# Expert weight loads spread over eight pairs, a second bank in the product chain of the last super block, and a new order in its first pair and routing

## The chip, the core and the metric

The kernel runs on one core of a Trainium2 chip. The metric is device time in microseconds (us) of one execution. The core's engines run side by side: TensorE (PE; its weight loads are shown as PEld), VectorE (DVE), ScalarE (ACT), GpSimd (POOL) and SyncE (SP), from which every transfer is issued, in one queue. PSUM has eight banks here, `bank[0]` to `bank[7]`, each 128 x 512 fp32.

## The reference

Three layers, one after the other, on 4 x 768 = 3072 tokens of 512 features:

```python
# attention: 8 heads of 64, chunks of 32 queries; each chunk sees 8 memory keys and a window of 56
scores = scale * np.matmul(q_c, k_full.transpose(0, 1, 3, 2))
a = np.exp(scores - np.max(scores, axis=-1, keepdims=True))
a = a / (np.sum(a, axis=-1, keepdims=True) + 1e-09)
out[:, :, c_start:c_end] = np.matmul(a, v_full)
# dense layer, 512 -> 2048 -> 512
r = np.maximum(x @ w_in, 0.0)
y = (s * (r * r) + b) @ w_out
# soft mixture, 8 experts of 4 slots, 512 -> 1024 -> 512
logits = y @ phi
d = softmax(logits, axis=0); slot_input = d.T @ y
slot_out[e] = np.maximum(slot_input[e] @ w1[e], 0.0) @ w2[e]
out = softmax(logits, axis=1) @ slot_out
```

(`softmax` stands for the lines that subtract the maximum, exponentiate and divide by the sum.) All is fp32.

## The kernel before

The 3072 tokens are six blocks of 512. Features lie on partitions, the tokens of a block on the free axis. Each fp32 operand of a large product is split into a high and a low part, and one product is three matmuls (high x high, high x low, low x high), all 128 x 128 by 128 x 512.

**Plain steps.** Blocks 0 and 1 run in 16 steps each, one 128-wide tile of the hidden layer a step: `mm_h` (12 matmuls, L332) into one of two banks, `make_g` (relu on ACT, times `s` on DVE, plus `b` on ACT, low part on DVE), then `mm_y` of the step before (`mm_job`, 12 matmuls, L351): three matmuls into each of four banks, which visits the banks in turn, four matmuls a round. The attention of later blocks runs between these as background tasks (`bg`, `run_bg`): `qk` (scores into a bank, then softmax on DVE and ACT), `tr` (transposes) and `pv`. The last four steps (`hand_step`) have their order written out.

**Super blocks.** Blocks 2 and 3, and 4 and 5, are done two at a time by `super_block(s, pending)`, s = 0 and 1, with seven products in place of eight (a 2 x 2 scheme over two blocks, two halves of the features and two hidden tiles). A *pair* p, 0 to 7, stands for hidden tiles p and p + 8. In it PE does, in this order:

- `a11` into bank A, copied by ACT to `c11`; `s1` into C, copied to `c22` (`y1n`, second half); `s2` accumulated on A, copied to `c12` (`y1n`, first half);
- in the first super block, `pv` of one attention unit in bank B and `qk` of the next in D;
- the first pending output job, 12 matmuls into the four banks `yp`;
- `s4` on C, added by DVE to `c12` (L768); `s3` on A, added by DVE to `c22` (L773); then relu (ACT, L677) and a 1024-wide multiplication (DVE, L680) make the hidden values of the second token block, which are kept for later;
- up to two routing tasks of the block before, in banks D and B: logits (`log`), transposes of y (`ytr0` to `ytr3`), of the exponents (`etr`), slot sums (`slot`); in pair 3 also `csoft`, a small softmax on DVE and ACT alone;
- the second pending job, 12 matmuls;
- `a22` on A, from which ACT and DVE make `t21` (`rt0n`, L677, L680); `a12` into B, which DVE adds to `c11` (L803), and `t11` follows; in the first super block then four transposes of the next attention unit into D.

Each product is six matmuls (`prod`, L662). The two jobs of a pair's own values are put on the pending list and run in the next pair; `finish(p - 1)`, at the start of the next pair, makes the last of those values, `G[0]`. The next pair's `a11` goes into A again, so it cannot start before `t21` has been made from A. Banks A, B, C, D are `yq`, `bank[4:8]` for s = 0 and `bank[0:4]` for s = 1; `yp` are the other four.

At the start `pending` holds what is left over: for s = 0 the last plain step's `mm_y` and the evacuation of `YB` (`evac_spare`, L372 on ACT and L370 on DVE, two banks each), for s = 1 the last two output jobs of s = 0, the second followed by an evacuation.

After the pairs, 16 output jobs of the second token block (`t2_job`) run into `yq`, with the routing of the first block between them. The first of the 16 visits the banks in the order D, C, A, B, one matmul each, three rounds.

**Transfers.** In the first super block the split operands of the products are also stored to DRAM (`wc_store`, `DWC`), and in the second they are loaded from there (`wc_load`, L617: `wi0n`, `wi1n`, `w14n`, `w15n`), five loads a pair with the weights of the output jobs (L602), each issued when its tile has been read for the last time. The expert weights (`e_load`, L494 and L496) are 64 loads of 512 KB in a fixed order, each started by `e_free` of some tile that is no longer needed. At the end of pair 0 of the second super block 13 tiles are freed at once, so 13 of these loads stand in SP's queue one behind the other, ahead of the pair's next loads.

PE's and SP's order is the order of the code throughout; that of ACT, DVE and POOL also, from the last four plain steps to the end of the super blocks.

Of the kernel before, what the change touches and what calls it, by code (L numbers as in the profile page):

```python
# [11 lines left out]
AF = mybir.ActivationFunctionType  # L12
# [4 lines left out]
NB = 6  # L17
# [21 lines left out]
def tile_attention_moe_softmoe(  # L39
# [287 lines left out]
    def mm_h(n, kts):  # L327
        w = WI[n % 2].rearrange("p (a k c) -> p a k c", a=2, k=4)
        for kt in kts:
            x = hl(X[(n // NF) % 2][kt])  # L330
            for i, (a, b) in enumerate(((0, 0), (0, 1), (1, 0))):
                pe.matmul(HB[n % 2], lhsT=r32(w[:, a, kt, :]), rhs=r32(x[:, b]),  # L332
                          start=(kt == 0 and i == 0), stop=(kt == 3 and i == 2))

    def make_g(n):
        r, t = hl(RT[n % 2])[:, 0], hl(RT[n % 2])[:, 1]
        g = hl(G[n % 2])
        act.activation(out=r, in_=HB[n % 2], func=AF.Relu, scale=1.0 / WSCALE ** 2)  # L338
        dve.scalar_tensor_tensor(out=t, in0=HB[n % 2], scalar=s_col, in1=r, op0=ALU.mult, op1=ALU.mult)  # L339
        act.activation(out=r32(g[:, 0]), in_=t, func=AF.Identity, bias=b_col)  # L340
        dve.scalar_tensor_tensor(out=r32(g[:, 1]), in0=t, scalar=b_col, in1=g[:, 0], op0=ALU.add,  # L341
                                 op1=ALU.subtract)

    def mm_job(yb, wt, gt, first, last, dts=(0, 1, 2, 3)):
        w, g = hl(wt), hl(gt)
        order = [(i, dt) for i in range(3) for dt in dts]
        if last:
            order.sort(key=lambda o: o[1])
        for i, dt in order:
            a, b = ((0, 0), (1, 0), (0, 1))[i]  # L350
            pe.matmul(yb[dt], lhsT=r32(w[:, a, dt * 128:dt * 128 + 128]), rhs=r32(g[:, b]),  # L351
                      start=(first and i == 0), stop=(last and i == 2))
# [27 lines left out]
    def y_logits(j, b):  # L380
        logit_mm(b)
        L = b[:, 0:128]
        old, new = mrun[(j + 1) % 2], mrun[j % 2]
        act.activation(out=lts, in_=L, func=AF.Copy)
        dve.tensor_reduce(out=new if j == 0 else st["mj"], in_=L, axis=AX.X, op=ALU.max)
        if j:
            dve.tensor_tensor(out=new, in0=st["mj"], in1=old, op=ALU.max)
            dve.tensor_tensor(out=st["da"], in0=old, in1=new, op=ALU.subtract)
            act.activation(out=st["aa"], in_=st["da"], func=AF.Exp)
        dve.tensor_scalar(out=st["nm"], in0=new, scalar1=-1.0, scalar2=None, op0=ALU.mult)  # L390
        act.activation(out=ets, in_=L, func=AF.Exp, bias=st["nm"],
                       accum_out=st["sj"] if j else srun)
        if j:
            dve.scalar_tensor_tensor(out=srun, in0=srun, scalar=st["aa"], in1=st["sj"], op0=ALU.mult,
                                     op1=ALU.add)

# [122 lines left out]
    for tasks in bg.values():  # L519
        tasks.sort(key=lambda t: t[0] != "pv")  # L520

    def run_bg(task, a, b=None):
        if task == "qk":
            att_qk(a, b)
            if a + 2 < NB * NHP:
                load_q(a + 2)
                load_k(a + 2)
            att_exp(a, b)
# [8 lines left out]
        elif task == "log":  # L537
            y_logits(a, b)
        elif task[:3] == "ytr":
# [139 lines left out]
    def times(out, h, r):  # L679
        dve.scalar_tensor_tensor(out=out, in0=h, scalar=s_col, in1=r, op0=ALU.mult, op1=ALU.mult)  # L680

    def super_block(s, pending):
        j1 = NPL + 2 * s
        yp, yq = (bank[0:4], bank[4:8]) if s == 0 else (bank[4:8], bank[0:4])
        A, B, C, D = yq
        ch = [fresh("y0"), fresh("y1")]
# [3 lines left out]
        jr = j1 - 1  # L690
        routing = {1: ("log", "ytr0"), 2: ("etr", "ytr1"), 3: ("ytr2", "ytr3"), 4: ("slot",)}
        gring = ["sp4", "sp5", "g1", "g0"] * 4
# [15 lines left out]

        def t2_job(i, dts=(0, 1, 2, 3)):
            mm_job(yq, cur[WR[i]], cur[gring[i]], i == 0, i == NF - 1, dts)  # L710

# [14 lines left out]
        for p in range(NPR):  # L726
            c11 = hl(ch[0])[:, p % 2]
            more = p + 1 < NPR
            prod(A, "a11", "b11", p)
            act.activation(out=c11, in_=A, func=AF.Copy)  # L730
            if s == 0 and p == 0:
                x_split("t4", 0, 1)
            if p:
                if s == 0:
                    att_place(4 * NHP + p, D)
                finish(p - 1)
            if s == 0:
# [19 lines left out]
            if s == 0:  # L757
                if p:
                    run_bg("pv", 4 * NHP + p, B)
                if more:  # L760
                    run_bg("qk", 4 * NHP + p + 1, D)
            pending.pop(0)()
            if p or s == 0:
                next_load(p, 0) if p else ws_load(R[3], 1)
            else:
                ws_load(R[2], NPR + 1)
# [5 lines left out]
            prod(A, "s3", "t3", p, False)  # L772
            dve.tensor_tensor(out=c22, in0=A, in1=c22, op=ALU.add)  # L773
            relu(r2, ch[1])
            times(cur[G2[p]], ch[1], r2)
            w_prep(2, p + 1)
            if not more:
                t2_load(4)
                prep(1)
                if s == 0:  # L780
                    x_split("t1", 1, 0)
                    x_split("t1", 1, 1)
            for i, t in enumerate(routing.get(p, ())):
                run_bg(t, jr, (D, B)[i])
            if p == 3:
                run_bg("csoft", jr)
            pending.pop(0)()
            if p:
                next_load(p, 1)
            elif s:  # L790
                ws_load(R[3], 1)
# [4 lines left out]
            relu(t21, A)  # L796
            times(t21, A, t21)
            prod(B, "a12", "b21", p)
            if s:
# [11 lines left out]
            pending.append(lambda p=p: mm_job(yp, cur[R[(2 * p + 1) % 4]], G[0], False, p == NPR - 1))  # L811
            if s and p == 0:
                for t in [cur[f"x0{h}"] for h in range(NHP)] + Q + K + V + PB + [EP]:
                    e_free(t)
# [39 lines left out]
        for i in range(NF):  # L854
            if s == 0 and i >= NF - 2:
                rest.append(lambda i=i: t2_job(i))
                continue
            t2_job(i, (3, 2, 0, 1) if i == 0 else (0, 1, 2, 3))
            if i == 0:
# [23 lines left out]
    with tc.manual_schedule(engines={mybir.EngineType.PE, mybir.EngineType.SP}):  # L883
# [61 lines left out]
        def plain_step(n):  # L945
# [3 lines left out]
            split_wo(n)  # L949
            mm_h(n, (3,) if n == 0 else (0, 1, 2, 3))  # L950
            make_g(n)
            if n + 2 < NF:
# [24 lines left out]
        def hand_step(n):  # L977
# [10 lines left out]
            if m == 3:  # L988
                w_split(1, 0)
            make_g(n)  # L990
            if n + 2 < NSTEP:
                split_wi(n + 2)
            for task, a in bg[n]:
                run_bg(task, a, bank[7] if n == NSTEP - 1 else HB[(n + 1) % 2] if task == "pv" else mbank())
            mm_y(n - 1)
# [16 lines left out]

        def evac_spare(yb):
            ybuf[:] = SPARE[0:4]
            y_evac(yb=yb)

        def last_job(job):
            job()
            evac_spare(bank[4:8])
# [253 lines left out]
```

## Time and profile before

| what | value |
|---|---|
| median of 3 runs | 685.29 us (684.33 to 685.44) |
| profiled execution, its own time | 685.56 us |
| its span | 683.8 us |
| PE busy | 656.8 us (96%) |
| DVE, ACT, POOL busy | 397.0, 329.3, 122.8 us |
| mean granted TensorE clock | 0.994 |
| bytes moved | 174.09 MB, 255 GB/s over the span |

The stages of the span: start and plain steps to 245 us, first super block 245 to 439, second 439 to 627, experts and output to the end.

How to read it: busy times say little where one engine is at 96%. What counts is where PE waits, and for whom. [...]

### The profile page before, as it was taken

The page shows a single profiled execution, that of the slowest core. Times are in us where ns is not written, and L with a number is a line of the kernel's source. Part 1 is how long each engine was busy: PE and PEld are TensorE (multiplying, and loading weights), DVE is VectorE, ACT ScalarE, POOL GpSimd, SP SyncE. Part 2 cuts the span into 40 slices and gives each one's busy share as a digit, 9 for nine tenths or more (in the row PEclk, how much of TensorE's full clock was granted, in tenths as well). Part 3 has the DMA queues.
Part 4 walks back from the last instruction along what each step waited for, and adds up shares of the span by engine and source line. Part 5 has one row for each costly group of instructions (what it writes and reads, how often), then busy time and mean ns, then how long its engine had stood idle before and what let it go on. Part 6 is the DMA issues. An engine that isn't in the chain of part 4 may idle for free.

```text
span 683.8 us, 12488 instructions
## 1 busy us (share of the span) xinstructions
PE 656.8 (96%) x4983; PEld 517.6 (76%) x4983; DVE 397.0 (58%) x707; ACT 329.3 (48%) x592; POOL 122.8 (18%) x118
## 2 busy tenths in 40 slices
PE   6899999999999999999999999997999999999995
PEld 4678888888878777787788787885787888877374
DVE  4799997665854686656555676244354444343333
ACT  3898885555545545555344553232243333323332
POOL 5100000233333565443353000000000000000000
PEclk9999999999999999999999999999999999999999
DMA  8999934575557667676764672479655567999887
GB/s 334 407 372 367 329 105 151 168 238 209 171 155 253 240 228 290 227 277 257 292 231 170 236 257 93 139 253 410 206 187 174 170 196 257 392 366 410 346 343 278
DMA packets 50745, 174.09 MB, mean 255 GB/s; under 512 B 5632, under 2 KB 5632, under 8 KB 50688
## 3 DMA queue, kind: packets, MB, share of 16 engines
q1 hardware_dynamic: 50688, 173.30, 70.0%
q8 instruction: 39, 0.64, 0.4%
q14 instruction: 18, 0.15, 0.1%
HBM read 139.72 MB, written 33.55 MB: 253 GB/s over the span
## 4 chain that ended last, share of the span: by engine, by line
PE 83%; DVE 7%; DMA 4%; ACT 3%; issue 1%; SPq 0%; DVEq 0%; POOL 0%; ACTq 0%; POOLq 0%
PE bank L351 36%; PE bank L662 18%; PE bank L332 11%; PE bank L198 3%; PE bank L247 3%; PE bank L1135 2%; PE bank L1094 2%; DMA k<-e1d 2%; PE bank L227 1%; DMA wi1n<-dwc 1%; PE bank L399 1%; DMA v<-vd 1%; DVE rt0n L680 1%; PE bank L415 1%; PE bank L1164 1%
## 5 line engine op out<-in xcount | busy, mean ns | idle before, releaser
L351 PE MATMUL bank<-g,wo 128*128 128x512 f32 x672 | 165.1, 396 | 0.0
L351 PEld LDWEIGHTS bank<-g,wo 128*128 128x128 f32 x672 | 123.5, 188 | 28.7 <-issue 1.7
L332 PE MATMUL bank<-x,wi 128*128 128x512 f32 x384 | 93.3, 391 | 0.7 <-ACT x03n L253 0.4
L332 PEld LDWEIGHTS bank<-x,wi 128*128 128x128 f32 x384 | 71.7, 188 | 16.4 <-ACT x03n L253 0.9
L677 ACT ACTIVATE rt1n<-y1n 128x1024 f32<-128x1024 f32 x16 | 17.0, 1061 | 78.7 <-DVE y1n L773 78.7
L1062 POOL MEMSET x10n<- 128x1024 f32 x1 | 1.0, 958 | 251.6 <-ACT ees L407 251.6
L339 DVE SCALAR_TENSOR_TENSOR rt<-bank,cons,rt 128x512 f32<-128x512 f32 x32 | 23.9, 747 | 33.8 <-ACT rt L338 33.8
L768 DVE TENSOR_TENSOR y1n<-bank,y1n 128x512 f32<-128x512 f32 x16 | 11.1, 691 | 55.4 <-PE bank L662 55.3
L316 POOL TENSOR_TENSOR wi<-w,wi 128x512 fp32r<-128x512 f32 x16 | 20.7, 1291 | 116.2 <-ACT wi L312 110.2
L324 ACT ACTIVATE wo<-w 128x512 fp32r<-128x512 f32 x32 | 20.2, 630 | 24.4 <-PE bank L351 13.8
L670 ACT ACTIVATE g<-rt0n,cons 128x512 fp32r<-128x512 f32 x32 | 23.2, 724 | 17.1 <-DVE rt0n L680 17.1
L325 POOL TENSOR_TENSOR wo<-w,wo 128x512 fp32r<-128x512 f32 x16 | 22.1, 1382 | 50.9 <-ACT wo L324 37.0
L312 ACT ACTIVATE wi<-w 128x512 fp32r<-128x512 f32 x32 | 20.1, 628 | 22.9 <-PE bank L332 20.3
L674 DVE SCALAR_TENSOR_TENSOR g<-rt0n,cons,g 128x512 fp32r<-128x512 f32 x32 | 24.2, 755 | 10.1 <-ACT g L670 9.7
L351 PE MATMUL bank<-g,yt0n 128*128 128x512 f32 x120 | 29.6, 396 | 0.0
L351 PE MATMUL bank<-g,yt1n 128*128 128x512 f32 x120 | 29.5, 395 | 0.0
L247 PEld LDWEIGHTS bank<-pb,v 128*64 128x64 f32 x704 | 22.3, 138 | 8.9 <-issue 3.2
L340 ACT ACTIVATE g<-rt,cons 128x512 fp32r<-128x512 f32 x32 | 23.1, 722 | 8.7 <-DVE rt L339 8.5
L341 DVE SCALAR_TENSOR_TENSOR g<-rt,cons,g 128x512 fp32r<-128x512 f32 x32 | 24.1, 752 | 5.4 <-ACT g L340 4.9
L198 PEld LDWEIGHTS bank<-k,q 128*64 128x64 f32 x704 | 23.1, 141 | 5.2 <-issue 4.3
L198 PE MATMUL bank<-k,q 128*64 128x64 f32 x704 | 25.7, 228 | 0.3 <-DMA k<-kd 0.3
L351 PEld LDWEIGHTS bank<-g,yt0n 128*128 128x128 f32 x120 | 22.1, 188 | 5.0 <-issue 0.4
(484 smaller groups left out, 1449.2 us busy)
## 6 DMA issues: line engine op xcount, KB each, us to landing
sp<-wd SPq DMA_DIRECT2D x24, 512.0 KB, 9.6
wo<-dws SPq DMA_DIRECT2D x24, 512.0 KB, 4.3
k<-kd SPq DMA_DIRECT2D x22, 512.0 KB, 7.6
v<-vd SPq DMA_DIRECT2D x22, 512.0 KB, 5.9
q<-qd SPq DMA_DIRECT2D x20, 512.0 KB, 6.7
dws<-wo SPq DMA_DIRECT2D x16, 512.0 KB, 6.7
yt0n<-dws SPq DMA_DIRECT2D x12, 512.0 KB, 6.0
yt1n<-dws SPq DMA_DIRECT2D x12, 512.0 KB, 3.7
```

Of the source, the lines that this page charges most:

```text
L198: pe.matmul(S[64 * par:64 * par + 64, 2 * i + z, :], lhsT=qt[:, c].rearrange("p h n -> p (h n)"), rhs=kt[:, c, :], start=True, stop=True)
L247: pe.matmul(b[64 * h:64 * h + 64, 64 * m:64 * m + 64], lhsT=vt[:, m, h, :], rhs=pb[:, m // 2, m % 2, h].rearrange("p z n -> p (z n)"), sta ...
L316: (dve if n < NF else pool).tensor_tensor(out=r32(t[:, 1]), in0=raw, in1=t[:, 0], op=ALU.subtract)
L325: (dve if n < NF else pool).tensor_tensor(out=r32(t[:, 1]), in0=raw, in1=t[:, 0], op=ALU.subtract)
L332: pe.matmul(HB[n % 2], lhsT=r32(w[:, a, kt, :]), rhs=r32(x[:, b]), start=(kt == 0 and i == 0), stop=(kt == 3 and i == 2))
L339: dve.scalar_tensor_tensor(out=t, in0=HB[n % 2], scalar=s_col, in1=r, op0=ALU.mult, op1=ALU.mult)
L340: act.activation(out=r32(g[:, 0]), in_=t, func=AF.Identity, bias=b_col)
L341: dve.scalar_tensor_tensor(out=r32(g[:, 1]), in0=t, scalar=b_col, in1=g[:, 0], op0=ALU.add, op1=ALU.subtract)
L351: pe.matmul(yb[dt], lhsT=r32(w[:, a, dt * 128:dt * 128 + 128]), rhs=r32(g[:, b]), start=(first and i == 0), stop=(last and i == 2))
L662: pe.matmul(b, lhsT=r32(wv[:, a, kt, :]), rhs=r32(xv[:, c]), start=(first and kt == 0 and i == 0), stop=(kt == 1 and i == 2), skip_group_c ...
L670: act.activation(out=r32(hl(dst)[:, 0]), in_=t, func=AF.Identity, bias=b_col)
L674: dve.scalar_tensor_tensor(out=r32(g[:, 1]), in0=t, scalar=b_col, in1=g[:, 0], op0=ALU.add, op1=ALU.subtract)
```

## The change

- **Expert loads.** The 13 tiles are freed two at the end of each pair of the second super block (`early[2 * p:2 * p + 2]`), in the same order: six times two and the last one alone.
- **Two banks.** In the second super block A and D change places in odd pairs, so `a11` goes into the bank that the pair before used as D. The routing's D moves with it.
- **First output job.** `t2_job(0)` does the three matmuls of a bank one after the other, and the banks in the order D, C, A, B (s = 0, as before) or, for s = 1, so that A and B, as they stand in pair 7, come last.
- **First pair.** The first pending job moves to the second place of the pair (an empty one stands in the first); for s = 0 the softmax of the attention unit in pair 0 comes after the two additions to `c12` and `c22`. The evacuation of the old output banks moves to the start of pair 1, behind `finish(0)`.
- **Routing.** `ytr0` comes before `log` in pair 1; the last DVE operation of `log` (`late`) comes after `t21`; `csoft` moves from pair 3 to the start of pair 5.
- **Hand steps.** `make_r` (the relu) is taken out of `make_g`, and a `pv` task runs between the two.

Nothing is computed otherwise, and no transfer is added or left out.

```diff
-    def mm_job(yb, wt, gt, first, last, dts=(0, 1, 2, 3)):
+    def mm_job(yb, wt, gt, first, last, dts=None):
         w, g = hl(wt), hl(gt)
-        order = [(i, dt) for i in range(3) for dt in dts]
-        if last:
-            order.sort(key=lambda o: o[1])
+        order = [(i, dt) for i in range(3) for dt in range(4)]
+        if last or dts:
+            order.sort(key=lambda o: dts.index(o[1]) if dts else o[1])
...
-        A, B, C, D = yq
+        B, C = yq[1:3]
...
-        routing = {1: ("log", "ytr0"), 2: ("etr", "ytr1"), 3: ("ytr2", "ytr3"), 4: ("slot",)}
+        routing = {1: ("ytr0", "log"), 2: ("etr", "ytr1"), 3: ("ytr2", "ytr3"), 4: ("slot",)}
+        early = [cur[f"x0{h}"] for h in range(NHP)] + Q + K + V + PB + [EP]
...
+        def t2_job(i):
+            mm_job(yq, cur[WR[i]], cur[gring[i]], i == 0, i == NF - 1,
+                   ((0, 2, 3, 1) if s else (3, 2, 0, 1)) if i == 0 else None)
...
         for p in range(NPR):
+            A, D = (yq[3], yq[0]) if s and p % 2 else (yq[0], yq[3])
             prod(A, "a11", "b11", p)
...
                 finish(p - 1)
+            if p == 1:
+                evac_spare(yp)
+            if p == 5:
+                run_bg("csoft", jr)
...
                 if more:
-                    run_bg("qk", 4 * NHP + p + 1, D)
+                    att_qk(4 * NHP + p + 1, D)
+                    att_next(4 * NHP + p + 1)
+                    if p:
+                        att_exp(4 * NHP + p + 1, D)
+                        att_norm(4 * NHP + p + 1)
             pending.pop(0)()
...
             dve.tensor_tensor(out=c22, in0=A, in1=c22, op=ALU.add)
+            if s == 0 and p == 0:
+                att_exp(4 * NHP + 1, D)
+                att_norm(4 * NHP + 1)
             relu(r2, ch[1])
...
-            if s and p == 0:
-                for t in [cur[f"x0{h}"] for h in range(NHP)] + Q + K + V + PB + [EP]:
+            if s:
+                for t in early[2 * p:2 * p + 2]:
                     e_free(t)
...
-            rest = super_block(0, [lambda: mm_y(NSTEP - 1), lambda: evac_spare(YB)])
-            super_block(1, [rest[0], lambda: last_job(rest[1])])
+            rest = super_block(0, [lambda: None, lambda: mm_y(NSTEP - 1)])
+            super_block(1, rest)
```

Three places show what moved. First SP's queue, second super block, end of pair 0 (`w14n`, `wi0n`, `wi1n`, `w15n` are product operands, `yt0n` and `yt1n` weights of output jobs, `e1d` the first expert layer's weights). Before:

```order
L617 DMA w15n_2445<-dwc1_144 128x1024
L494 DMA x00n_1330<-e1d 128x1024
L494 DMA x01n_1331<-e1d 128x1024
L494 DMA x02n_1332<-e1d 128x1024
...
L494 DMA ep_111<-e1d 128x1024
L617 DMA wi0n_2354<-dwc3_146 128x512
L617 DMA wi1n_2373<-dwc2_145 128x1024
L602 DMA yt0n_2182<-dws10_137 128x1024
```

Now:

```order
L626 DMA w15n_2445<-dwc1_144 128x1024
L500 DMA x00n_1330<-e1d 128x1024
L500 DMA x01n_1331<-e1d 128x1024
L626 DMA wi0n_2354<-dwc3_146 128x512
L626 DMA wi1n_2373<-dwc2_145 128x1024
L611 DMA yt0n_2182<-dws10_137 128x1024
L626 DMA w14n_2418<-dwc2_145 128x1024
L611 DMA yt1n_2184<-dws2_129 128x1024
L626 DMA w15n_2445<-dwc2_145 128x1024
L500 DMA x02n_1332<-e1d 128x1024
L500 DMA x03n_1333<-e1d 128x1024
```

Two expert loads, not 13, now stand ahead of `wi0n` and `wi1n`.

Second PE, the same super block, from pair 2 to pair 3 (`w15n` gives `a22` and `a12`, `wi0n` gives `a11`). Before:

```order
L662 MATMUL bank0_175<-w6n_3807,w15n_2445 128x512 x3
L662 MATMUL bank0_175<-w13n_3965,w15n_2445 128x512 x3
L662 MATMUL bank1_176<-w1n_3703,w15n_2445 128x512 x3
L662 MATMUL bank1_176<-w8n_3707,w15n_2445 128x512 x3
L662 MATMUL bank0_175<-w0n_3544,wi0n_2354 128x512 x3
```

Now:

```order
L671 MATMUL bank0_175<-w6n_3807,w15n_2445 128x512 x3
L671 MATMUL bank0_175<-w13n_3965,w15n_2445 128x512 x3
L671 MATMUL bank1_176<-w1n_3703,w15n_2445 128x512 x3
L671 MATMUL bank1_176<-w8n_3707,w15n_2445 128x512 x3
L671 MATMUL bank3_178<-w0n_3544,wi0n_2354 128x512 x3
```

The next pair's first product goes into bank 3 instead of bank 0.

Third DVE, first super block, pair 0 (`ep` is the attention softmax, `y1n` the sums `c12` and `c22`, `x10n` the second block's hidden values, `sp0`, `sp1` evacuated outputs, `rt0n` is `t21`). Before:

```order
L580 TENSOR_TENSOR w13n_2438<-x01n_1331,w13n_2438 128x512
L211 MEMSET bank7_182 64x8
...
L221 TENSOR_TENSOR ep_111<-ep_111,ast1_172 128x512
L768 TENSOR_TENSOR y1n_2424<-bank6_181,y1n_2424 128x512
L773 TENSOR_TENSOR y1n_2424<-bank4_179,y1n_2424 128x512
L680 SCALAR_TENSOR_TENSOR x10n_2427<-y1n_2424,cons_66,rt1n_2426 128x1024
L370 TENSOR_SCALAR sp0_112<-bank1_176 128x512
L370 TENSOR_SCALAR sp1_113<-bank3_178 128x512
L680 SCALAR_TENSOR_TENSOR rt0n_2425<-bank4_179,cons_66,rt0n_2425 128x512
```

Now:

```order
L589 TENSOR_TENSOR w13n_2438<-x01n_1331,w13n_2438 128x512
L792 TENSOR_TENSOR y1n_2424<-bank6_181,y1n_2424 128x512
L797 TENSOR_TENSOR y1n_2424<-bank4_179,y1n_2424 128x512
L211 MEMSET bank7_182 64x8
...
L221 TENSOR_TENSOR ep_111<-ep_111,ast1_172 128x512
L689 SCALAR_TENSOR_TENSOR x10n_2427<-y1n_2424,cons_66,rt1n_2426 128x1024
L689 SCALAR_TENSOR_TENSOR rt0n_2425<-bank4_179,cons_66,rt0n_2425 128x512
```

The two sums go ahead of the softmax, and the evacuation is gone from between `x10n` and `rt0n`.

## Rows read from the trace of the kernel before

**Rows 1.** Waits of PE: line, releaser, us in total, times, longest.

```profile
PE bank L662 <- DMA wi1n<-dwc: 4.6, 1, 4.6
...
PE bank L662 <- DVE rt0n L680: 2.7, 8, 0.8
...
PE bank L662 <- DVE y1n L773: 0.8, 1, 0.8
PE bank L662 <- DVE sp L403: 0.8, 1, 0.8
...
PE bank L332 <- ACT x03n L253: 0.4, 1, 0.4
```

**Rows 2.** Timeline of SP's issues, second super block: start, us, instruction.

```profile
454.80 0.38 SPq L494 DMA_DIRECT2D x00n<-e1d  x1
...
465.75 0.33 SPq L494 DMA_DIRECT2D ep<-e1d  x1
...
468.20 0.33 SPq L617 DMA_DIRECT2D wi1n<-dwc  x1
...
498.50 0.32 SPq L617 DMA_DIRECT2D wi1n<-dwc  x1
```

**Rows 3.** Timeline of PE, pair 2 of the second super block.

```profile
472.34 0.86 PE L662 MATMUL bank<-w7n,wi0n 128*128 128x512 f32 x3
477.82 1.65 PE L662 MATMUL bank<-w2n,wi1n 128*128 128x512 f32 x3 [4.62 <-DMA wi1n<-dwc]
...
482.17 2.88 PE L351 MATMUL bank<-g,wo 128*128 128x512 f32 x12
```

**Rows 4.** Engines by stretch: us, busy of PE, PEld, DVE, ACT, POOL; granted clock, DMA, GB/s.

```profile
478.00:482.00 4.00, 4.00 (x12) 3.14 (x13) 0.00 (x0) 0.60 (x1) 0.00 (x0) 0.62 0.94 371
...
391.00:439.00 48.00, 47.90 (x247) 38.11 (x248) 28.34 (x51) 20.18 (x37) 0.00 (x0) 1.00 0.50 169
```

**Rows 5.** Timeline of PE, end of pair 5 and start of pair 6, second super block.

```profile
541.49 0.84 PE L662 MATMUL bank<-w8n,w15n 128*128 128x512 f32 x3
542.50 0.97 PE L662 MATMUL bank<-w0n,wi0n 128*128 128x512 f32 x3 [0.17 <-DVE rt0n L680]
543.31 0.85 PE L662 MATMUL bank<-w7n,wi0n 128*128 128x512 f32 x3
```

**Rows 6.** Timeline of PE, pair 0 of the first super block: `s3`, `a22`, next `a11`.

```profile
254.25 0.84 PE L662 MATMUL bank<-w5n,w14n 128*128 128x512 f32 x3
...
256.55 0.98 PE L662 MATMUL bank<-w6n,w15n 128*128 128x512 f32 x3 [0.79 <-DVE y1n L773]
...
260.88 0.96 PE L662 MATMUL bank<-w0n,wi0n 128*128 128x512 f32 x3 [0.83 <-DVE rt0n L680]
```

**Rows 7.** Timeline of DVE, first super block, pair 0 (to 261 us) and pair 2.

```profile
255.80 0.69 DVE L773 TENSOR_TENSOR y1n<-bank,y1n 128x512 f32<-128x512 f32 x1
257.68 1.28 DVE L680 SCALAR_TENSOR_TENSOR x10n<-y1n,cons,rt1n 128x1024 f32<-128x1024 f32 x1 [1.19 <-ACT rt1n L677]
258.88 1.28 DVE L370 TENSOR_SCALAR sp<-bank 128x512 f32<-128x512 f32 x2
260.08 0.74 DVE L680 SCALAR_TENSOR_TENSOR rt0n<-bank,cons,rt0n 128x512 f32<-128x512 f32 x1
...
287.74 0.07 DVE L211 MEMSET bank<- 64x8 f32 x1 [2.21 <-PE bank L198]
...
291.26 0.69 DVE L221 TENSOR_TENSOR ep<-ep,ast 128x512 f32<-128x512 f32 x1
```

**Rows 8.** Timeline of PE and DVE, start of pair 1, second super block.

```profile
454.47 0.96 PE L662 MATMUL bank<-w0n,wi0n 128*128 128x512 f32 x3
...
457.42 0.75 DVE L674 SCALAR_TENSOR_TENSOR g<-rt0n,cons,g 128x512 fp32r<-128x512 f32 x1 [0.79 <-ACT g L670]
```

**Rows 9.** Timeline of PE, first output jobs after the pairs: first and second super block.

```profile
390.01 0.61 PE L351 MATMUL bank<-sp4n,sp6n 128*128 128x512 f32 x2
...
393.75 5.60 PE L351 MATMUL bank<-g,wo 128*128 128x512 f32 x24
...
573.03 3.31 PE L351 MATMUL bank<-sp4n,sp6n 128*128 128x512 f32 x12
```

More of the change, by code (lines that the diff above doesn't have):

```diff
@@ L333, in mm_h, with make_r @@
                           start=(kt == 0 and i == 0), stop=(kt == 3 and i == 2))
+    def make_r(n):
+        act.activation(out=hl(RT[n % 2])[:, 0], in_=HB[n % 2], func=AF.Relu, scale=1.0 / WSCALE ** 2)
     def make_g(n):
@@ L337, in make_g @@
         g = hl(G[n % 2])
-        act.activation(out=r, in_=HB[n % 2], func=AF.Relu, scale=1.0 / WSCALE ** 2)
         dve.scalar_tensor_tensor(out=t, in0=HB[n % 2], scalar=s_col, in1=r, op0=ALU.mult, op1=ALU.mult)
@@ L392, in y_logits, with late @@
                        accum_out=st["sj"] if j else srun)
-        if j:
-            dve.scalar_tensor_tensor(out=srun, in0=srun, scalar=st["aa"], in1=st["sj"], op0=ALU.mult,
-                                     op1=ALU.add)
+        def late():
+            if j:
+                dve.scalar_tensor_tensor(out=srun, in0=srun, scalar=st["aa"], in1=st["sj"], op0=ALU.mult,
+                                         op1=ALU.add)
+        return late
     def y_tr(tt, b, eng):
@@ L520, in tile_attention_moe_softmoe, with att_next @@
         tasks.sort(key=lambda t: t[0] != "pv")
+    def att_next(a):
+        if a + 2 < NB * NHP:
+            load_q(a + 2)
+            load_k(a + 2)
     def run_bg(task, a, b=None):
@@ L524, in run_bg @@
             att_qk(a, b)
-            if a + 2 < NB * NHP:
-                load_q(a + 2)
-                load_k(a + 2)
+            att_next(a)
             att_exp(a, b)
@@ L537, in run_bg @@
         elif task == "log":
-            y_logits(a, b)
+            y_logits(a, b)()
         elif task[:3] == "ytr":
@@ L680, in times, with evac_spare @@
         dve.scalar_tensor_tensor(out=out, in0=h, scalar=s_col, in1=r, op0=ALU.mult, op1=ALU.mult)
+    def evac_spare(yb):
+        ybuf[:] = SPARE[0:4]
+        y_evac(yb=yb)
     def super_block(s, pending):
@@ L707, in t2_load @@
             ws_load(WR[i], i // 2 + NPR * (i % 2), i in (0, 6, 7, 8, 9))
-        def t2_job(i, dts=(0, 1, 2, 3)):
-            mm_job(yq, cur[WR[i]], cur[gring[i]], i == 0, i == NF - 1, dts)
+        def t2_job(i):
+            mm_job(yq, cur[WR[i]], cur[gring[i]], i == 0, i == NF - 1,
+                   ((0, 2, 3, 1) if s else (3, 2, 0, 1)) if i == 0 else None)
         def next_load(p, k):
@@ L760, in super_block @@
                 if more:
-                    run_bg("qk", 4 * NHP + p + 1, D)
+                    att_qk(4 * NHP + p + 1, D)
[3 more added lines that the diff above has]
+                        att_norm(4 * NHP + p + 1)
             pending.pop(0)()
-            if p or s == 0:
-                next_load(p, 0) if p else ws_load(R[3], 1)
-            else:
+            if p:
+                next_load(p, 0)
+            elif s:
                 ws_load(R[2], NPR + 1)
@@ L782, in super_block @@
                     x_split("t1", 1, 1)
[L783 to L786, printed above, removed]
+            late = lambda: None
+            for t in routing.get(p, ()):
+                if t == "log":
+                    late = y_logits(jr, D)
+                else:
+                    run_bg(t, jr, B if t in ("ytr0", "ytr1", "ytr3") else D)
             pending.pop(0)()
@@ L789, in super_block @@
                 next_load(p, 1)
-            elif s:
+            else:
                 ws_load(R[3], 1)
@@ L797, in super_block @@
             times(t21, A, t21)
+            late()
             prod(B, "a12", "b21", p)
@@ L857, in super_block @@
                 continue
-            t2_job(i, (3, 2, 0, 1) if i == 0 else (0, 1, 2, 3))
+            t2_job(i)
             if i == 0:
@@ L950, in plain_step @@
             mm_h(n, (3,) if n == 0 else (0, 1, 2, 3))
+            make_r(n)
             make_g(n)
@@ L989, in hand_step @@
                 w_split(1, 0)
+            make_r(n)
+            tasks = [lambda t=t, a=a: run_bg(t, a, bank[7] if n == NSTEP - 1 else HB[(n + 1) % 2] if t == "pv" else mbank())
+                     for t, a in bg[n]]
+            if bg[n][0][0] == "pv":
+                tasks.pop(0)()
             make_g(n)
@@ L992, in hand_step @@
                 split_wi(n + 2)
-            for task, a in bg[n]:
-                run_bg(task, a, bank[7] if n == NSTEP - 1 else HB[(n + 1) % 2] if task == "pv" else mbank())
+            for t in tasks:
+                t()
             mm_y(n - 1)
@@ L1011, in hand_step @@
                 ws_load(R[2], NPR + 1)
[L1013 to L1019, printed above, removed]
         for n in range(NSTEP - 4):
```

## The prediction

> **What bounds the kernel now.** The page comes first: PE is busy for 656.8 of 683.8 us, and no other engine for more than 397. So the change can only win time in which PE stands still or runs slowly, and PE's waits are the next view. They name one long wait, 4.6 us for a transfer into `wi1n`, and below it a family of short ones for DVE and ACT at the joints of the pairs [rows 1]. The other long entries of that view lie in the start and the tail, which the change does not touch.
>
> A wait is worth more than its idle time. The reader is to measure from start to start. A row of 12 matmuls is recorded as 2.88 us and one of 24 as 5.60 [rows 3, 9], so 12 more take 2.72 us: 0.227 each, 0.68 for a group of three. From pair 5 to pair 6 of the second super block the first group of `a11` starts 1.01 us after the last one of `a12`, and the next group 0.81 us after that [rows 5]: 1.82 where 1.36 would do, a loss of 0.46 us behind an idle entry of 0.17. So a short wait costs its entry plus about 0.3 us.
>
> **The change part by part.** The profiled execution took 685.56 us, 0.27 more than the median of the runs shown; the sum is made against it.
>
> *Expert loads.* SP issues the first of the 13 at 454.80 and the last at 465.75, and the load of `wi1n` that pair 2 needs only at 468.20 [rows 2]; in a pair without the burst it is issued at 498.50, some 4 us after its pair has begun. The 13 are issued on average 0.9 us apart, the last ones slower than the first, because the transfers cannot keep up. Pair 2 stops: from 472.34 to 482.17 PE does five groups of three, 3.40 us of work, in 9.83 us [rows 3]. [...] With two loads ahead of it, about 2 us of transfers, `wi1n` is issued when its tile is free and lands many microseconds before its use. I take the whole 6.4 us. What hides the moved loads is the slack of each pair's own loads, a pair of 66 matmuls, 15 us, between issue and use. Nobody needs the expert tiles before the second super block is over, and all 13 are still loaded by then (six times two and one).
>
> *Two banks.* With `a11` in the other bank, PE no longer waits for `t21`. Seven joints at 0.46 us give 3.2 us. What is late next is `s2`, which accumulates on the new bank and needs ACT's copy of `a11` from it: six matmuls of `s1`, 1.36 us, lie between, and the copy comes one relu after `t21`; I cost it at nothing, since PE gains only 0.3 us on it.
>
> *First output jobs.* In the first super block 12 matmuls take from 390.01 to 393.75, 3.74 us for 2.72; in the second the row is 3.31 long and not 2.88 [rows 9]. Three matmuls a bank, with the late banks last, put six matmuls (1.36 us) before A and nine before B. That covers both: 1.0 + 0.4 = 1.4 us.
>
> *Hand step.* `pv`'s copy to `x03n` stood behind `g` on ACT, which waited for DVE; PE lost 0.4 + 0.3 = 0.7 us [rows 1]. Put ahead of `g`, it needs nothing but its own matmuls. `g` comes 0.6 us later, and its reader is the `mm_y` of the next step, behind 12 matmuls.
>
> *Routing.* In pair 1 PE waited for the copy of `ytr0` behind the small operations of `log`, in pair 3 for `t21` behind `csoft`: entries of 0.8 and 0.8 [rows 1], 1.05 us each, 2.1 together. `csoft` in pair 5 falls into the 2.2 us that DVE idles before the attention of each pair [rows 7]; its exponent blocks ACT until DVE is ready, and the copies queued behind it are of banks that PE wants a job later.
>
> *First pair, first super block.* Two waits stand here, for `c22` and for `t21`: 256.55 follows 254.25 by 2.30 instead of 1.36, and 260.88 comes late by about as much [rows 6]. The edit takes away the first; the second is DVE's own chain, and the question is what is left of it. With `mm_y` behind it `s3` starts 2.7 us earlier, near 251.5, ends near 253.0, and the sum to `c22` ends 0.7 later, 253.7. Then the softmax, 4.2 us by pair 2 (287.74 to the end of the row at 291.26), `x10n` 1.28 and `rt0n` 0.74 [rows 7]: 259.9. Pair 1 starts there and not at 260.88, a gain of 0.9 us. PE would be ready at 258.7, so a wait of some 1.2 us remains. The bounds are 2.2 (no wait left) and 0.2 (the softmax slowed as it would be beside POOL's work).
>
> *Evacuation in pair 1.* 1.28 us on DVE for two banks [rows 7]. In the first super block it fits into the same 2.2 us gap: nothing. In the second it stands behind the last operation of `finish`, which began at 457.42, 2.95 after the pair [rows 8], and does not move with PE. So it ends near 459.4, while the first output job into these banks comes 18 matmuls after `a11`, which now starts 0.4 us earlier: 458.2. The second bank is wanted at 458.4 and free at 458.8, the fourth at 459.3 and 459.4. I take a cost of 0.5, between 0 (the job's own order hides it) and 1.3 (the whole evacuation).
>
> The sum: 6.4 + 3.2 + 1.4 + 0.7 + 2.1 + 0.9 - 0.5 = 14.2 us. Against the profiled 685.56 that is 671.3, and 671.0 for the median.
>
> [...] The output jobs visit four banks in turn, a different one each matmul, and in a stretch that is full of them (391 to 439 us) the granted clock is 1.00 [rows 4]. [...] The sum goes by the row.
>
> **The rivals.**
>
> - *DVE takes over in the first super block.* The waits there are only passed on: the orders differ, DVE's work does not. For it: one of its two waits in pair 0 survives by my own working. Against it: from pair to pair DVE has idle time. Then routing, pair 0 and the first block's output job give nothing (4.0 us): 675.0.
> - *The spare bank is not spare.* D carries the routing in pairs 1 to 4; if its readers on ACT and DVE are late, `a11` waits for them instead, and the 3.2 us stay: 674.2. Against it: the routing's output job lies between, 2.7 us.
> - *`wi1n` is late for another reason.* If the burst only stood beside the real cause, the 6.4 stay: 677.4. Against it: the issue time follows the burst directly [rows 2].
> [...]
> - *Slower: every pair waits for its weights.* Two expert loads stand in the same queue before the five loads of each next pair. If they and the pair's own loads together did not land within a pair, seven pairs would each lose the 6.4 us that one loses now: 685.3 + 6 x 6.4 - 7.8, about 716. It decides when the delay reaches the 9.6 us from the issue of `wi1n` at 468.20 to its use [rows 2, 3]; two loads amount to about 2.
>
> **How the numbers follow.** Forecast 0.60, DVE 0.22, spare bank 0.06, another reason 0.06, clock 0.02, slower 0.02, and 0.02 for something unnamed that leaves the time where it is. A measurement of this kernel can tell about 0.2%, 1.4 us, from no change. All cases but the last two are faster: 0.96, 0.02, 0.02. The range goes down to 669.2 (all of pair 0's 2.2, no cost of the evacuation), rounded to 669.0, and up over DVE and spare bank to 675.5; it leaves out the others, 0.12, and the rare meeting of two cases.
>
> **What would show it.** Right: no wait for `wi1n`, no stretch of granted clock below 1 between the start and the tail, SP's issue of `wi1n` early in each pair; no entries of `rt0n` in the second super block; `a12` to `a11` there 0.68 us apart; a wait of about a microsecond for `rt0n` left after pair 0 of the first; a wait of the first output job of pair 1 for `sp` L372's banks in the second. Wrong: a wait for any `dwc` or `dws` load, or for an expert tile; entries for `rt0n` as many as before; the stages before 200 us or after 627 us of another length.

## The result, and the profile after

| | before | after |
|---|---|---|
| median, us | 685.37 (684.33 to 685.68, 4 runs) | 673.93 (672.41 to 674.23, 4 runs) |
| profiled execution, its span | 685.56, 683.8 | 673.84, 672.0 |
| PE busy | 656.8 us | 653.4 us |
| mean granted TensorE clock | 0.994 | 0.993 |

The ratio is 0.983, 95% interval 0.981 to 0.985: 11.4 us faster, inside the predicted range, 2.9 us short of the predicted 671.0. Waits of PE in the kernel after (line, releaser, us in total, times, longest; the first line lies before 200 us and stands for all the waits there):

```profile
PE bank L198 <- ACT q L184: 3.3, 1, 3.3
PE bank L671 <- DVE rt0n L689: 2.1, 1, 2.1
...
PE bank L353 <- DVE sp L372: 0.2, 1, 0.2
```

Against [rows 1] the waits for `wi1n`, `y1n`, `sp` L403 and `x03n` are gone, and of the eight for `rt0n` one is left. That one is new in size: 2.1 us. Pair by pair, from the start of the first `a11` group to the next pair's (the last one to the first output job), in us:

| pair | 0 | 1 | 2 | 3 | 4 | 5 | 6 | 7 |
|---|---|---|---|---|---|---|---|---|
| first super block, before | 16.10 | 20.39 | 18.39 | 19.60 | 18.96 | 17.70 | 17.69 | 16.40 |
| after | 16.23 | 20.99 | 18.40 | 18.86 | 18.92 | 17.70 | 17.69 | 16.40 |
| second super block, before | 15.23 | 17.07 | 22.55 | 16.32 | 16.66 | 15.43 | 15.43 | 15.10 |
| after | 14.96 | 17.26 | 15.68 | 15.85 | 16.19 | 14.96 | 14.96 | 14.95 |

The second super block gives 133.79 - 124.81 = 8.98 us, the pairs of the first nothing (145.23 and 145.19): what pair 3 gains, pairs 0 and 1 lose. The other gains lie in the start (`a11` of pair 0 starts at 243.20, not 244.78) and in the first output jobs. First the places that went as forecast. SP's issues of the kernel after, second super block:

```profile
452.17 0.38 SPq L500 DMA_DIRECT2D x00n<-e1d  x1
452.64 0.38 SPq L500 DMA_DIRECT2D x01n<-e1d  x1
...
455.84 0.33 SPq L626 DMA_DIRECT2D wi1n<-dwc  x1
```

With two expert loads ahead of it and not 13 [rows 2], `wi1n` is issued 14.3 us before the group at 470.18 that reads it, and pair 2 runs through, as the timeline of PE after shows with the other places of the second super block:

```profile
455.64 0.39 PE L353 MATMUL bank<-g,yt0n 128*128 128x512 f32 x1
456.19 2.94 PE L353 MATMUL bank<-g,yt0n 128*128 128x512 f32 x11 [0.16 <-DVE sp L372]
458.97 0.84 PE L671 MATMUL bank<-w3n,w14n 128*128 128x512 f32 x3
...
469.50 0.84 PE L671 MATMUL bank<-w7n,wi0n 128*128 128x512 f32 x3
470.18 0.84 PE L671 MATMUL bank<-w2n,wi1n 128*128 128x512 f32 x3
...
472.90 2.88 PE L353 MATMUL bank<-g,wo 128*128 128x512 f32 x12
...
530.82 0.84 PE L671 MATMUL bank<-w8n,w15n 128*128 128x512 f32 x3
531.50 0.84 PE L671 MATMUL bank<-w0n,wi0n 128*128 128x512 f32 x3
...
561.41 2.88 PE L353 MATMUL bank<-sp4n,sp6n 128*128 128x512 f32 x12
564.13 5.60 PE L353 MATMUL bank<-g,wo 128*128 128x512 f32 x24
```

The five groups from `w7n` to the job take 472.90 - 469.50 = 3.40 us, where they took 9.83 [rows 3]. `a12` to `a11` is 0.68, where it was 1.01 [rows 5]. The first output job takes 2.72. And the job of pair 1 takes 458.97 - 455.64 = 3.33 for 2.72: the evacuation's price, 0.61.

What went wrong is pair 0 of the first super block. PE there, after:

```profile
256.76 0.60 PE L227 MATMUL bank<-cons,ep 128*128 128x128 f32 x4
259.43 1.52 PE L671 MATMUL bank<-w0n,wi0n 128*128 128x512 f32 x3 [2.06 <-DVE rt0n L689]
260.74 1.48 PE L671 MATMUL bank<-w7n,wi0n 128*128 128x512 f32 x3
262.02 1.31 PE L671 MATMUL bank<-w2n,wi1n 128*128 128x512 f32 x3
263.17 0.86 PE L671 MATMUL bank<-w9n,wi1n 128*128 128x512 f32 x3
```

The wait for `c22` is gone, but the one for `t21` grew from 0.83 [rows 6] to 2.06, and the three groups behind it take 3.74 us, not some 2.2. The reason for the slow groups is the granted clock (columns as in [rows 4]):

```profile
258.00:262.00 4.00, 2.57 (x6) 2.03 (x7) 3.80 (x5) 1.25 (x2) 3.84 (x4) 0.70 1.00 390
...
436.00:564.00 128.00, 127.84 (x602) 104.36 (x601) 55.70 (x82) 46.10 (x76) 0.00 (x0) 1.00 0.73 243
```

From 258 to 262 it is 0.70; by the microsecond, 258 to 259 has 1.00, 259 to 260 has 0.80, and each of the three from 260 to 263 has 0.50. PE had stood still for 2.06 us just before. DVE of the kernel after over the same place:

```profile
250.22 0.69 DVE L792 TENSOR_TENSOR y1n<-bank,y1n 128x512 f32<-128x512 f32 x1 [2.29 <-PE bank L671]
251.51 0.69 DVE L797 TENSOR_TENSOR y1n<-bank,y1n 128x512 f32<-128x512 f32 x1 [0.60 <-PE bank L671]
252.28 0.07 DVE L211 MEMSET bank<- 64x8 f32 x1
...
255.79 0.69 DVE L221 TENSOR_TENSOR ep<-ep,ast 128x512 f32<-128x512 f32 x1
256.40 2.30 DVE L689 SCALAR_TENSOR_TENSOR x10n<-y1n,cons,rt1n 128x1024 f32<-128x1024 f32 x1
258.63 0.74 DVE L689 SCALAR_TENSOR_TENSOR rt0n<-bank,cons,rt0n 128x512 f32<-128x512 f32 x1
```

and POOL (the operation on `wi1n` has the same form):

```profile
251.11 1.31 POOL L663 TENSOR_TENSOR wi1n<-sp6n,wi1n 128x512 fp32r<-128x512 f32 x1
256.14 1.48 POOL L663 TENSOR_TENSOR w14n<-sp6n,w14n 128x512 fp32r<-128x512 f32 x1 [3.73 <-ACT w14n L662]
```

DVE stands idle for 2.29 and 0.60 us, then runs the whole softmax, and only then `x10n`, which takes 2.30 instead of 1.28 [rows 7]: POOL's operation had begun 0.26 us earlier.

### The profile page after: what moved, and what is told of

Read it like the earlier page. It is cut to its first block, busy times and chain, and to the rows that moved or that the text cites. A ratio compares the mean times of both kernels' runs of the same rounds, so it can differ in the third digit from the quotient of the medians.

```text
span 672.0 us, 12487 instructions
## 1 busy us (share of the span) xinstructions
PE 653.4 (97%) x4983; PEld 518.7 (77%) x4983; DVE 397.1 (59%) x707; ACT 328.3 (49%) x592; POOL 123.3 (18%) x118
## 4 chain that ended last, share of the span: by engine, by line
PE 92%; DVE 4%; ACT 2%; issue 1%; DVEq 0%; POOL 0%; ACTq 0%; POOLq 0%
PE bank L353 39%; PE bank L671 22%; PE bank L332 11%; PE bank L247 4%; PE bank L198 4%; PE bank L1163 2%; PE bank L1122 2%; PE bank L227 2%; PE bank L405 2%; PE bank L379 1%; PE bank L421 1%; PE bank L1192 1%; PE bank L927 1%; DVE w L301 0%; ACT sp L295 0%
## 5 line engine op out<-in xcount | busy, mean ns | idle before, releaser
L689 DVE SCALAR_TENSOR_TENSOR rt0n<-bank,cons,rt0n 128x512 f32<-128x512 f32 x16 | 12.0, 750 | 25.8 <-ACT rt0n L686 25.8
```

## The experiments

Each ran on a chip beside the kernel before; its ratio is to those runs. Kernel before: 686.70 median on the chip of experiments 1 to 4, 685.52 on that of 5 to 8, 686.17 on that of 9 to 12 (9 runs each). Diffs are against the changed kernel where nothing else is said.

**1. All 13 loads in one burst again.**

```diff
-            if s:
-                for t in early[2 * p:2 * p + 2]:
+            if s and p == 0:
+                for t in early:
```

> The changed kernel with all 13 expert loads back at the end of pair 0 of the second super block, everything else as changed. Theory (the burst is the cause of the long wait, and spreading it was worth 6.4 us): 6.4 us slower than the changed kernel's 673.9, so about 680.3; a wait of some 4.6 us for wi1n in pair 2 and 3.4 us of low clock after it. Rival (the burst only stood beside the cause, or the two banks and the new order hide most of it): 674 to 676.

681.15 us, ratio 0.992 (0.991 to 0.993). SP's issues and PE of this run:

```profile
452.44 0.38 SPq L500 DMA_DIRECT2D x00n<-e1d  x1
...
463.64 0.33 SPq L500 DMA_DIRECT2D ep<-e1d  x1
464.97 0.33 SPq L626 DMA_DIRECT2D wi0n<-dwc  x1
466.25 0.33 SPq L626 DMA_DIRECT2D wi1n<-dwc  x1
```

```profile
475.88 1.65 PE L671 MATMUL bank<-w2n,wi1n 128*128 128x512 f32 x3 [5.25 <-DMA wi1n<-dwc]
```

Pair 2 takes 22.97 us instead of 15.68, the others what they take without the burst: the 7.3 us lie in this pair alone.

**2. One bank again in the second super block.**

```diff
-                   ((0, 2, 3, 1) if s else (3, 2, 0, 1)) if i == 0 else None)
+                   (3, 2, 0, 1) if i == 0 else None)
...
-            A, D = (yq[3], yq[0]) if s and p % 2 else (yq[0], yq[3])
+            A, D = yq[0], yq[3]
```

> The changed kernel with the product chain of the second super block in one bank again. Theory (seven joints at 0.46 us): 3.2 us slower than the changed kernel, about 677.1, with a wait of 0.17 us for rt0n at each joint. Rival (the second bank only moves the wait to s2 or to the routing, and is worth nothing): 673.9.

676.42 us, ratio 0.985 (0.983 to 0.986). PE's waits for `rt0n` are seven again:

```profile
PE bank L671 <- DVE rt0n L689: 3.1, 7, 2.1
```

The second super block's pairs take 127.77 instead of 124.81 us, 2.96 more: 0.47 to 0.51 in pairs 2 to 6, 0.28 in pair 0 and 0.15 in pair 7, but only 0.06 in pair 1, where the wait for `sp` L372 goes in exchange. So the joints give back about 3.4 us, of which 0.45 returns in pair 1, where the first output job takes 2.88 and not 3.33: the evacuation's wait exists because PE arrives earlier. The trace carries this reading; by the ratios alone the two kernels lie 1.1 us apart, with overlapping intervals.

**3. Softmax ahead of the sums, as before, in pair 0.**

```diff
-                    if p:
-                        att_exp(4 * NHP + p + 1, D)
-                        att_norm(4 * NHP + p + 1)
+                    att_exp(4 * NHP + p + 1, D)
+                    att_norm(4 * NHP + p + 1)
...
-            if s == 0 and p == 0:
-                att_exp(4 * NHP + 1, D)
-                att_norm(4 * NHP + 1)
```

> The changed kernel with the softmax of pair 0 of the first super block ahead of the two sums again, as before the change; the evacuation and the output job stay where the change put them. Theory (in the changed order DVE stands idle for 2.3 us before the first sum and is late for t21 by 2.1 us, at which the clock falls, another 1.7 us): softmax first fills that gap; the wait for t21 and the low clock after it go, a wait of about 0.9 us for the sum to c22 comes back: about 671. Rival (the prediction's view that the sums must go first): 0.9 us or more slower, 674.8 to 676.

670.52 us, ratio 0.976 (0.975 to 0.978). Pair 0 takes 14.66 us and not 16.23: a wait of 0.5 for `c22`, none for `rt0n`, and the first three groups of pair 1 take 2.17 us (258.60 to 260.77), not 3.74. This part of the change was a loss. The other two edits of this pair, the output job in the second place and the evacuation taken out, are worth 16.10 - 14.66 = 1.44 us by themselves.

**4. Eight dead matmuls in PE's wait** (they write bank C, which is free there; the result is not read).

```diff
+            if s == 0 and p == 0:
+                for _ in range(8):
+                    pe.matmul(C, lhsT=r32(wop("a12", p)[:, 0, 0, :]), rhs=r32(xo("b21", 0)[:, 0]), start=True, stop=True)
```

> The changed kernel with eight more matmuls at the end of pair 0 of the first super block, into bank C, whose result nothing reads: they stand in the 2.1 us in which PE waits for t21. Theory (the wait lets the clock fall): pair 1 starts no later, its first groups run at 0.68 us instead of 1.3, the granted clock stays 1.00: about 672.2. Rival A (the clock falls for another reason): 673.9 with the low clock still there. Rival B (the matmuls lie on the path): 1.8 us slower, 675.7.

672.58 us, ratio 0.980 (0.979 to 0.981). PE's timeline:

```profile
257.31 2.10 PE L842 MATMUL bank<-w1n,w15n 128*128 128x512 f32 x8
259.62 0.96 PE L671 MATMUL bank<-w0n,wi0n 128*128 128x512 f32 x3 [0.21 <-DVE rt0n L689]
...
261.80 0.84 PE L671 MATMUL bank<-w9n,wi1n 128*128 128x512 f32 x3
```

and its engines by stretch (columns as in [rows 4]):

```profile
258.00:262.00 4.00, 3.79 (x17) 2.79 (x16) 3.80 (x5) 1.93 (x4) 3.84 (x4) 1.00 1.02 389
```

`a11` starts as late as without them, but its first three groups take 2.18 us and not 3.74, at a granted clock of 1.00. Work that computes nothing kept the clock up: pair 1 takes 19.39 us and not 20.99, so 1.6 us of the loss is the clock's.

**5. The changed kernel once more**, beside the next three.

> The changed kernel itself, as the mark for the other runs of this chip. All theories: between 672.4 and 674.3 where the kernel before takes 685.4, a ratio of 0.983; its executions differ by 1.7 us among themselves if the clock falls after the wait in pair 0 in some of them only.

673.72 us (671.85 to 674.13), ratio 0.982 (0.980 to 0.984). The wait is 2.07 us, pair 0 takes 16.22 and pair 1 21.03. Of its runs and the four first ones, the two with a mean granted clock of 0.995 and 0.996 took 671.85 and 672.41, the six at 0.991 to 0.993 took 673.38 to 674.23. It may be that the clock does not fall in every execution, but this is not shown: all six profiles with this wait (the changed kernel's two and those of runs 1, 2, 9 and 10) have the slow pair 1, 20.99 to 21.04 us, and the mean clock varies in the kernel before as well, which has no such wait (0.987 at 687.50 us, 0.994 at 684.82).

**6. POOL's operation later.**

```diff
-            w_prep(2, p + 1)
+            if s or p:
+                w_prep(2, p + 1)
...
+            if s == 0 and p == 0:
+                w_prep(2, p + 1)
```

(the second one stands behind `t21`)

> The changed kernel with the split of one weight tile (w14n, ACT and POOL) of pair 0 of the first super block put behind t21 instead of ahead of it. Theory (x10n took 2.30 us and not 1.28 because POOL worked on two SBUF operands beside it): x10n back at 1.3 us, the wait for rt0n 1.0 us instead of 2.1, about 1.0 us faster than the changed kernel, and 2.7 if the clock then does not fall. Rival (x10n is slow by itself there, or POOL's work is needed soon): unchanged, or slower with a new wait for w14n in pair 1.

670.80 us, ratio 0.979 (0.977 to 0.980). PE's wait is 1.04, pair 0 takes 15.20 us, and the clock stays at 1.00 from 258 to 262. DVE:

```profile
256.19 1.28 DVE L689 SCALAR_TENSOR_TENSOR x10n<-y1n,cons,rt1n 128x1024 f32<-128x1024 f32 x1
```

and POOL:

```profile
256.57 2.02 POOL L663 TENSOR_TENSOR w14n<-sp6n,w14n 128x512 fp32r<-128x512 f32 x1 [4.37 <-ACT w14n L662]
```

The two still overlap, but now DVE begins first, by 0.38 us, and it is POOL that takes longer. So 1.02 of the wait was `x10n` behind POOL, and the 1.04 that remain bring no fall of the clock. The 15.20 us are 0.9 less than the 16.10 before: with `x10n` at its 1.28, pair 0 gains exactly what was forecast for it. Both together are 2.6 us; the medians differ by 2.9.

**7. Softmax split around the sums**: maximum, difference and exponent ahead of them, sum and division behind.

```diff
+                    att_exp(4 * NHP + p + 1, D)
                     if p:
-                        att_exp(4 * NHP + p + 1, D)
...
-                att_exp(4 * NHP + 1, D)
                 att_norm(4 * NHP + 1)
```

> The changed kernel with the softmax of pair 0 cut in two: maximum, difference and exponent ahead of the two sums, the sum over the keys and the division behind them. Theory (the gap of 2.3 us on DVE is filled and neither sum comes late): no wait for the sum to c22, a wait for t21 of 0 to 0.6 us, no low clock; 3.0 to 4.0 us faster than the changed kernel. Rival (DVE's work in pair 0 is too long in any order): like the order with the softmax first, 2.5 to 3 us faster, no more.

669.89 us, ratio 0.977 (0.975 to 0.978). Pair 0 takes 13.91 us: 2.19 less than before, the upper bound of the prediction, and no wait is left in it. DVE and POOL:

```profile
254.39 1.28 DVE L689 SCALAR_TENSOR_TENSOR x10n<-y1n,cons,rt1n 128x1024 f32<-128x1024 f32 x1
```

```profile
254.46 2.35 POOL L663 TENSOR_TENSOR w14n<-sp6n,w14n 128x512 fp32r<-128x512 f32 x1 [1.53 <-ACT w14n L662]
```

This time DVE begins 0.07 us earlier and keeps its 1.28; POOL takes 2.35, and PE does not wait for it.

**8. The kernel before with the loads spread, and nothing else.**

```diff
-            if s and p == 0:
-                for t in [cur[f"x0{h}"] for h in range(NHP)] + Q + K + V + PB + [EP]:
+            if s:
+                for t in ([cur[f"x0{h}"] for h in range(NHP)] + Q + K + V + PB + [EP])[2 * p:2 * p + 2]:
```

(against the kernel before)

> The kernel before with one part of the change alone: the 13 expert loads two at the end of each pair. Theory (worth 6.4 us by itself, independent of the rest): 6.4 us faster than the kernel before, ratio 0.9907. Rival (its worth depends on the second bank and the new order, which change what SP waits for): 4 us or less, or a new wait for a dwc or dws load.

678.64 us, ratio 0.990 (0.988 to 0.991): 6.9 faster. The second super block's pairs take 127.41 instead of 133.79, 6.4 less; the other waits are those of [rows 1].

**9. Seven loads in pair 0 and six in pair 1.**

```diff
-                for t in early[2 * p:2 * p + 2]:
+                for t in early[7 * p:7 * p + 7]:
```

> Seven expert loads in pair 0 and six in pair 1 of the second super block, the rest as changed. Slack theory (the prediction's): a burst costs only what exceeds the 9.6 us from the issue of wi1n to its use; seven loads, some 0.9 us apart, delay wi1n by about 6.5, so no wait for wi1n appears and the time is that of the changed kernel, 673.8 (672.5 to 675). Rival, that any burst costs in proportion: half of the 7.3 us that the burst of 13 cost, 677.5, with a wait for wi1n.

672.0 us (671.62 to 673.25), ratio 0.979 (0.978 to 0.981), not slower than the changed kernel, and its second super block takes 124.83 us, as with two a pair. No wait for `wi1n`: that a burst costs only what exceeds the slack holds, and the rival is out. (The median is 1.9 us below the changed kernel's while the pairs of the profiles agree, so that difference is not shown to come from the loads.) SP's issues, the landing of this `wi1n` and its reader on PE:

```profile
451.95 0.38 SPq L500 DMA_DIRECT2D x00n<-e1d  x1
...
456.83 0.33 SPq L626 DMA_DIRECT2D wi1n<-dwc  x1
```

```profile
DMA to landing us min/median/max: 10.6/10.6/10.6
```

```profile
469.98 0.84 PE L671 MATMUL bank<-w2n,wi1n 128*128 128x512 f32 x3
```

and the landing of the one issued at 455.84 in the changed kernel:

```profile
DMA to landing us min/median/max: 4.7/4.7/4.7
```

Counted from the first expert load, `wi1n` is issued only 1.2 us later than with two (4.88 against 3.67): the first loads are issued about 0.5 us apart, and in run 1 the last ones follow each other at 1.3. But it takes 10.6 us to land and not 4.7. So it is there at 467.4 instead of 460.5, about as late as I expected, and 2.6 us before its use. The delay shows in the landing and not in the issue.

**10. Evacuation ahead of `finish`**, second super block.

```diff
+                if s and p == 1:
+                    evac_spare(yp)
                 finish(p - 1)
-            if p == 1:
+            if p == 1 and s == 0:
                 evac_spare(yp)
```

> The changed kernel with the evacuation of pair 1 in the second super block ahead of the last operation of finish. If DVE's order there costs PE what the traces read, 0.6 us (3.33 for a row of 2.72), the time is 673.2 and the wait for sp L372 is gone. Rival: finish ends 1.3 us later and its reader waits instead, 673.8 or more.

673.03 us, ratio 0.980 (0.978 to 0.983): too near the changed kernel to tell by the median. PE:

```profile
455.98 2.88 PE L353 MATMUL bank<-g,yt0n 128*128 128x512 f32 x12
458.70 0.84 PE L671 MATMUL bank<-w3n,w14n 128*128 128x512 f32 x3
```

The job takes 2.72 and waits for nothing, and nobody waits for `finish`: the 0.6 us are shown in the trace.

**11 and 12. The best version: 7 and 10 together, and with 6 as well.**

> Softmax split around the sums in the first pair, plus the early evacuation, POOL untouched. If both gains add: 669.9 - 0.6 = 669.3, no entry of PE's waits left between the start and the tail above 0.3 us. Rival: the evacuation only moves DVE's lateness on, 669.9.

> As the run before with POOL's splitting of w14n behind the rest of pair 0 as well. If x10n beside POOL no longer decides once the softmax is early, the same as the run before, 669.3 (within 1). Rival: with x10n undisturbed PE gains another 0.3 to 1.

Without 6: 669.01 us (668.78 to 669.37), ratio 0.975 (0.973 to 0.977); with it 669.43, ratio 0.976 (0.974 to 0.977). The first beats both kernels: 17 us faster than before, and below the changed kernel's 0.982 (0.980 to 0.984). The view of PE's waits lists none in the two super blocks, and pair 0 of the first super block takes 13.90 us, pair 1 of the second 16.66. POOL's operation needs no other place once DVE begins first.

## Why the prediction was right, and where it was not

- *Expert loads*, 6.4 us: 9.83 - 3.40 = 6.43, and 6.4 in the pairs of run 8. Right, and for the reason given: run 1 brings the wait back by the burst alone, run 9 shows that a delay within the slack costs nothing. One reading was wrong: the 9.6 us from the issue of `wi1n` to its use are no slack. PE was waiting for the load in the last 4.6 of them, and they are its landing time behind the burst. The slack of the changed kernel, from the landing at 460.5 to the use at 470.18, is 9.6 as well, which is luck. The average of 0.9 us between issues hid that the first ones pass much faster (0.48 from the first, at 454.80, to the second).
- *Two banks*, 3.2: the joints of the second super block are 0.68 now; pairs 3 to 6, in which nothing else changes, gain 0.47 each, so seven joints 3.3 (3.2 by the sum of the pairs), and run 2 gives them back. `s2` waits for nothing.
- *First output jobs*, 1.4: 3.74 - 2.72 = 1.02 and 3.15 - 2.72 = 0.43 (before, the second one ran from 573.03 [rows 9] to 576.18). *Hand step*, 0.7: the two rows of 12 took 234.82 - 228.47 = 6.35 us, as PE's timeline before has them:

```profile
228.47 3.02 PE L351 MATMUL bank<-g,wo 128*128 128x512 f32 x12
...
234.82 0.60 PE L227 MATMUL bank<-cons,ep 128*128 128x128 f32 x4
...
576.18 5.61 PE L351 MATMUL bank<-g,wo 128*128 128x512 f32 x24
```

They take 233.25 - 227.67 = 5.58 now, 0.77 less:

```profile
227.67 3.02 PE L353 MATMUL bank<-g,wo 128*128 128x512 f32 x12
230.52 2.89 PE L332 MATMUL bank<-x,wi 128*128 128x512 f32 x12
233.25 0.60 PE L227 MATMUL bank<-cons,ep 128*128 128x128 f32 x4
```

- *Routing*, 2.1: pair 3 gives 0.74 and not 1.05, since 0.27 of its wait stays (it is gone in runs 3, 6 and 7 and in the best version, where pair 3 takes 18.58 or 18.59; why is open); pair 1 gives 1.01 as run 7 shows it (19.38 us against 20.39), where no slow clock lies over it. Together 1.75.
- *Evacuation in pair 1*, -0.5: -0.61, taken back by run 10.
- *First pair, first super block*, +0.9: **this step failed.** Pair 0 lost 0.13 us, and pair 1 another 1.6: -1.7, so 2.6 us below the term, about what the sum lacks (14.2 forecast, 11.7 in the profiled executions). The working held up to `x10n`: from the pair's start the sum to `c22` ends at 9.0 us (forecast 253.7, from 244.78 8.9), and the softmax takes 4.2. The order itself was not weighed against the old one: run 3 shows that softmax first, with the other edits, costs only 0.5 of waiting. Then two things came that had no term. First, `x10n` was costed at 1.28 and took 2.30. I had thought of POOL for the lower bound, but put its price on the softmax: in pair 0 of the kernel before, its L219 took 0.97 us, from 253.27, beside POOL's operation on `wi1n` (252.93 to 254.21), and in pair 2 it took 0.17. Both operations follow on ACT: the relu into `rt1n` releases `x10n`, the copy into `w14n` right behind it releases POOL. In the kernel before, DVE stood waiting for `rt1n` and began `x10n` at 257.68 [rows 7], ahead of POOL's operation, which then took 1.87:

```profile
258.25 1.87 POOL L654 TENSOR_TENSOR w14n<-sp6n,w14n 128x512 fp32r<-128x512 f32 x1 [4.03 <-ACT w14n L653]
```

Now DVE is in the softmax until 256.48, and POOL begins first, at 256.14. Run 6 takes exactly this 1.02 back. Of `x10n` and POOL's operation the one that begins second takes longer, in both directions: DVE 2.30 here, POOL 2.35 in run 7. Second, the wait left over was 2.06 and not 1.2 us, and behind it the granted clock was 0.70 from 258 to 262: 1.6 us, by run 4. I had written that no stretch below 1 would be left, and took no price for what a longer wait does.

With -1.74 in place of 0.9, the terms as measured are 6.43 + 3.2 + 1.45 + 0.77 + 1.75 - 1.74 - 0.61 = 11.25. The profiled executions differ by 11.72. The rest, 0.5, is the start ahead of the hand steps, which was 0.8 us shorter in this execution (pair 0 of the changed kernel began at 243.20 here and at 243.81 in its second profile), less 0.25 in the tail. A start before 200 us of another length was named as a sign of being wrong; with the same code ahead of it, pair 0 begins anywhere from 242.99 to 243.94 in the profiles of this document, so I take this 0.8 for scatter, and nothing here tests it.

Of the rivals, *DVE takes over* is nearer in time, 675.0 against the measured 673.9, than the forecast's 671.0, and the range covered both; so the number alone does not speak for the forecast. The parts do: the rival was right on one pair, the one my own working had named, and wrong on the rest, since the routing gave 1.75 us and the first block's output job 1.02, which it had put at nothing. The spare bank was spare: no `a11` of the second super block waits. The clock did cost something, the 1.6 us behind the wait in pair 0 of the first super block, but the second bank cost none: from 436 to 564 us, with two banks in turn, the granted clock is 1.00. And no pair waits for weights.

## What to carry to other kernels

When two operations change places on an engine, ask what that engine does while it waits for the first one: here DVE idled 2.3 us ahead of the sums, and the best order was neither of the two but half a softmax, the sums, the other half. A wait that stays should be priced with what follows it, since here a wait of 2.06 us on PE cost 1.6 more in clock and one of 1.04 (run 6) nothing. A burst of prefetches cost nothing where the just-in-time load behind it still landed before its use: with seven loads 2.6 us before (run 9). Look at the landing and not at the issue: behind seven loads the issue was 1.2 us later, the landing 7.

## What the hardware showed that I had not expected

- After a standstill of 2.06 us that followed four short transposes, the granted clock was 0.70 from 258 to 262 us, with 0.50 from 260 to 263; after 1.04 us (run 6) it was 1.00 from 258 to 262, and with eight matmuls in the gap (run 4) it was 1.00 as well.
- Of `x10n` on DVE and the operation on `w14n` on POOL, the one that began second took longer in each of these profiles, even when it began only 0.07 us later. Where POOL began 0.26 earlier, DVE took 2.30 for 1.28; where DVE began 0.07, 0.38 or 0.57 earlier (runs 7 and 6, the kernel before), DVE kept its 1.28 and POOL took 2.35, 2.02 or 1.87, against 1.31 on `wi1n`.
- SP issued the first loads of the burst about 0.5 us apart and the last ones 1.3 apart (452.44 and 452.91, 464.97 and 466.25 in run 1); in both kernels with the burst `wi1n` came 9.6 us after its issue (468.20 to 477.82 [rows 2, 3] and 466.25 to 475.88), behind seven loads 10.6, behind two 4.7.
